# An attention and mixture-of-experts kernel: the first expert's weights get a room of their own and are fetched in the last pairs, the last pair is worked in two query halves, the last routing and the first swaps move forward

## The chip, the core and the metric

The kernel runs on one core of one Trainium2 chip. The core has five engines with a queue each: TensorE (PE in the rows; its weight loads are PEld), VectorE (DVE), ScalarE (ACT), GpSimd (POOL) and SyncE (SP), which here only issues transfers. They work in parallel and wait for each other by semaphores. Every engine's instructions run in the order in which they were written. PE writes to PSUM, the other engines read it; everything else lives in SBUF. The metric is the device time of one launch in microseconds (us). PE's clock has two levels, 2.4 and 1.2 GHz; "granted clock" 1.00 in a row is the upper, 0.50 the lower.

## What is computed

```python
B, H, S, D = q.shape                       # 8, 8, 576, 64
scores = scale * np.matmul(q, k.transpose(0, 1, 3, 2))
kth = np.partition(scores, -32, axis=-1)[..., -32:-31]
scores = np.where(scores >= kth, scores, -1e9)
attn = softmax(scores)
x = (attn @ v).transpose(0, 2, 1, 3).reshape(B * S, H * D)     # 4608 x 512
do = x @ w_skip > 0
logits = x[do] @ w_gate                    # 8 experts
e = argmax(logits); gate = softmax(logits)[e]
y = gate * (relu(x[do] @ w1[e]) @ w2[e])   # w1 512 x 1024, w2 1024 x 512
out = x;  out[do] = x[do] + y
```

## The kernel before

**Attention.** Two heads are a pair; there are `NP` = 32 pairs, four to a batch. A pair's 576 query rows are nine row tiles of 64 rows with both heads side by side (`NR` = 9; tile 8 is the remainder). Its steps, with lines:

- `load_raw`, `load` (L79 to 84, L487): SP loads raw k and q; `load_v` (L497 to 508): SP loads V twice, as `VG` for the values and as `vraw` for the gate.
- `prep` (L541): PE transposes raw into PSUM, ACT copies it to `TT` (L563, L565, "put"), and SP copies halves of `TT` into `TS` with the heads' partitions exchanged ("swap", L581 for k, L583 for q). Row tiles with an odd number take their operands from `TS`, the even ones from `TT`.
- `rows` (L604): PE forms scores (L616), two row tiles to a PSUM tile `r`; ACT copies them to `XC` (L641; tile 8 L643; remainder columns L625).
- `row`, per row tile: DVE takes the top eight of seven chunks (L683) and ranks candidates (L689, L691) to get a first threshold `cl`; ACT writes signs (L696); POOL pushes the wanted scores to `xw` (L699, "push") and fills its end (L703); DVE takes the maxima of that window (L712, "window"), of which the eighth is the exact threshold `wn`; the mask row `PEN` is written by ACT (L709) or, for tiles 2 and 6, by POOL (L707, `PENS`).
- `units` (L742): per 128 keys PE forms the scores again, transposed (L757), and adds the masks (L750); ACT takes the exponential into `PTM` (L788; remainders L791, L794). Every unit waits for all nine mask rows of the pair.
- `heads` (L808): PE multiplies with V (L831, L838); DVE divides by the sums (L841, L867, L844) and adds to the router's logits (L848 to L854); SP stores the result twice (L888, L889), in the last pair ACT's queue does.

**Routing.** When a group of batches (0 to 3, 4 to 6, 7) is ready, `route` (L354 to 478) computes skip, expert, gate and rank of each token with many small operations, then one-hots (`rrh` L459 to L464, `rlo` L468), and PE turns them into the token lists (L474), which DVE adds to `LS` (L477).

**Experts.** `make_room` (L1038) opens the tiles of the first expert in space that the attention gives back. Then, for expert 0, SP fetches four quarters of w1 (`fetch`, L927, 512 KB each) and later four of w2 into the raw tiles; each quarter is split into a rounded high part by ACT (`part_hi`, L930) and a low part, raw less high, by POOL for w1 and DVE for w2 (`part_lo`, L933). POOL gathers the tokens (L994); `turning` transposes them on PE (L1013), ACT rounds (L1017), DVE forms the low part (L1021). An up-product (L1076 to L1078) or down-product (L1099 to L1101) is three matmuls, high by high, low by high and high by low; ACT and DVE apply relu between them (L1081, L1084). The first two blocks of 128 tokens (`EARLY`) start before the last group is routed, with 224 columns; the third follows the last list with 128 columns. The other experts run in a loop behind that.

**Order.** A planner (`Plan`, L150 to 262) writes the instructions. Every task has an engine, an estimated duration, tasks that it needs, and a due number; `when(p, kind, j)` = 9p + `K[kind]` + `FINE[kind][j]`. The planner simulates the engines; of the tasks that could start first on an engine it takes the one with the smallest due number, and waits up to `LOOK` of a duration for a task that is `GAIN` more urgent. The first run of the planner orders the attention, the first two routings, and the first expert's w1 and tokens up to `turning`; the second run (`pl.run()` after L1112) orders the last routing, both blocks' products and the w2 parts.

## Time and profile before

| | before |
|---|---|
| runs | 1092.0, 1093.87, 1099.29 us (median 1093.87) |
| the profiled execution | 1102.62 us, span 1100.7 us, mean granted clock 0.961 |
| PE | 1028.4 us busy (93%) |
| DVE | 907.6 us busy (82%) |
| ACT | 862.4 us busy (78%) |
| POOL | 717.2 us busy (65%) |

Busy shares are means over stages with different limits: attention until about 800 us, experts behind it. All times within the kernel are counted from the start of the span. In a row of the timeline, "x4" means four like instructions in a run; "[2.88 <-DVE hl L1084]" means that the engine was idle for 2.88 us before and that the work named released it. `SPq` and `ACTq` are issues of transfers on these queues; "(xN)" in a window is the number of instructions that touch it.

### The profile page before, as it was taken

What the parts mean: (1) busy time and instruction counts of PE and PEld (TensorE: products, weight loads), DVE (VectorE), ACT (ScalarE), POOL (GpSimd) and SP (SyncE); (2) the same over time, 40 slices, a digit from 0 to 9 for tenths busy, and PEclk for the clock granted to TensorE, in tenths of its full rate; (3) what the DMA queues carried; (4) which work ended last, traced back from release to release, by engine and by line L of the source; (5) the groups of instructions that cost most, each with busy time, mean ns of one, the idle gap of its engine ahead of it and who ended that gap; (6) DMA issues with size and microseconds to landing.
All of it is one profiled execution on the core that took longest, in us unless ns stands there. A gap on an engine that the chain in (4) does not pass through costs nothing.

```text
span 1100.7 us, 40070 instructions
## 1 busy us (share of the span) xinstructions
PE 1028.4 (93%) x14912; PEld 731.9 (66%) x14912; DVE 907.6 (82%) x4910; ACT 862.4 (78%) x1542; POOL 717.2 (65%) x1079
## 2 busy tenths in 40 slices
PE   6799999999999999999999999998868799999996
PEld 3366666666666666666666666665648798889995
DVE  3999999999999999999999999997844365675661
ACT  4899999999999999999999999997842244334450
POOL 2778787888788878888688999887970131111111
PEclk9799999999999999999999999998987689999998
DMA  5333434444443444444344443432147265455620
GB/s 112 88 69 84 95 83 97 105 94 94 96 91 83 104 103 97 90 94 90 83 103 96 96 94 89 99 83 51 40 136 228 68 202 168 145 172 183 202 85 28
DMA packets 290092, 116.15 MB, mean 106 GB/s; under 512 B 258920, under 2 KB 275304, under 8 KB 289888
## 3 DMA queue, kind: packets, MB, share of 16 engines
q1 hardware_dynamic: 282288, 103.13, 38.5%
q0 software_dynamic: 3360, 9.47, 2.5%
q8 instruction: 119, 1.95, 0.7%
q10 hardware_dynamic: 4240, 0.90, 0.4%
q14 instruction: 85, 0.70, 0.2%
HBM read 76.91 MB, written 24.53 MB: 92 GB/s over the span
## 4 chain that ended last, share of the span: by engine, by line
PE 39%; DVE 33%; POOL 13%; ACT 7%; issue 4%; DMA 3%; SPq 1%; POOLq 0%; ACTq 0%; DVEq 0%
DVE cand L683 12%; DVE wn L712 9%; POOL xw L699 7%; PE r L616 4%; DVE cand L691 4%; DVE cl L689 4%; PE r L757 4%; PE ph L1076 4%; PE ph L1077 4%; PE ph L1078 4%; PE py L1099 4%; PE py L1101 4%; PE py L1100 4%; ACT r L696 3%; POOL xw L703 3%
## 5 line engine op out<-in xcount | busy, mean ns | idle before, releaser
L699 POOL TENSOR_TENSOR xw<-XC,r 128x576 f32<-128x576 f32 x288 | 365.2, 1283 | 98.8 <-ACT r L696 72.5
L683 DVE MAX8 cand<-XC 128x8 f32<-128x82 f32 (+1 forms) x2016 | 362.1, 229 | 19.1 <-ACT XC L641 18.8
L712 DVE MAX8 wn<-xw 128x8 f32<-128x585 f32 x288 | 215.5, 760 | 24.4 <-POOL xw L703 21.2
L696 ACT ACTIVATE r<-XC,cl 128x576 bf16<-128x576 f32 x288 | 224.5, 788 | 5.1 <-DVE cl L689 4.1
L616 PE MATMUL r<-TT 64*64 64x64 f32 (+1 forms) x1280 | 203.6, 432 | 0.2 <-ACT PTM L788 0.2
L709 ACT ACTIVATE PEN<-XC,wn 128x576 bf16<-128x576 f32 x224 | 170.2, 785 | 7.7 <-DVE wn L712 7.4
L616 PE MATMUL r<-TS 64*64 64x512 f32 (+1 forms) x1024 | 169.1, 425 | 3.7 <-DMA TS<-TT 3.7
L757 PE MATMUL r<-TT 64*128 64x512 f32 x512 | 150.1, 664 | 16.1 <-ACT XC L643 13.3
L689 DVE MAX8 cl<-cand 128x8 f32<-128x28 f32 (+2 forms) x864 | 153.0, 191 | 0.8
L788 ACT ACTIVATE PTM<-r,top 128x1024 f32<-128x1024 f32 x128 | 140.4, 1125 | 6.4 <-PE r L750 6.2
L641 ACT ACTIVATE XC<-r 128x1024 f32<-128x1024 f32 x128 | 132.1, 1035 | 14.6 <-PE r L616 14.4
L930 ACT ACTIVATE hi<-raw 128x1024 fp32r<-128x1024 f32 x64 | 67.4, 1056 | 74.4 <-PE py L1101 60.9
L750 PEld LDWEIGHTS <-PEN 64*128 64x128 bf16 (+1 forms) x2880 | 70.9, 100 | 76.7 <-issue 74.1
L933 DVE TENSOR_TENSOR lo<-raw,hi 128x1024 fp32r<-128x1024 f32 x60 | 73.5, 1224 | 54.1 <-ACT hi L930 53.5
L707 POOL TENSOR_SCALAR PEN<-XC,wn 128x576 bf16<-128x576 f32 x64 | 110.9, 1733 | 9.2 <-DVE wn L712 4.5
L703 POOL TENSOR_SCALAR xw<-wo,CN 128x9 f32<-128x9 f32 x288 | 99.3, 345 | 26.0
L691 DVE MATCH_REPLACE8 cand<-cl,cand 128x28 f32<-128x28 f32 (+1 forms) x576 | 101.7, 180 | 0.0
L1076 PE MATMUL ph<-xh,hi 128*128 128x224 f32 (+4 forms) x288 | 92.1, 320 | 8.8 <-DVE xb L844 5.9
L1077 PE MATMUL ph<-xl,hi 128*128 128x224 f32 (+4 forms) x288 | 91.5, 318 | 0.3 <-DVE xl L1021 0.3
L1078 PE MATMUL ph<-xh,lo 128*128 128x224 f32 (+4 forms) x288 | 91.3, 317 | 0.0
L994 POOL DMA_INDIRECT xg<-xd,idx x21 | 24.6, 1171 | 101.4 <-DVE ot L1000 87.5
L831 PEld LDWEIGHTS pt<-VG,PTM 128*64 128x64 f32 x2112 | 73.1, 137 | 23.5 <-issue 12.3
(264 smaller groups left out, 2072.2 us busy)
## 6 DMA issues: line engine op xcount, KB each, us to landing
raw<-in_moe_w_dram SPq DMA_DIRECT2D x64, 512.0 KB, 3.8
TS<-TT SPq DMA_DIRECT2D x64, 144.0 KB, 2.5
raw<-in_k_dram SPq DMA_DIRECT2D x64, 128.0 KB, 2.9
VG<-in_v_dram SPq DMA_DIRECT2D x64, 128.0 KB, 2.6
vraw<-in_v_dram SPq DMA_DIRECT2D x64, 128.0 KB, 2.6
raw<-in_q_dram SPq DMA_DIRECT2D x62, 128.0 KB, 3.2
xd<-xb SPq DMA_DIRECT2D x62, 128.0 KB, 2.4
out_dram<-xb SPq DMA_DIRECT2D x62, 128.0 KB, 2.4
```

The costliest lines, as they stand in the source:

```text
L616: nc.tensor.matmul(o[hs_(h)], q_, (ts[src, u:w] if y else tt[src, 0, u:w]), start=True, stop=True)
L683: nc.vector.max(C_[:, c], xc[:, CH[c]:CH[c + 1]])
L689: nc.vector.max(L[:, 4 * r:4 * r + 8], c)
L691: nc.vector.match_replace(c, L[:, 4 * r - 4:4 * r + 4], c, LOWEST)
L696: nc.scalar.activation(rr_, xc, AF.Sign, bias=CL[p % 2][:, t, 23:24], scale=-ODD, accum_out=CN[:, s:s + 1])
L699: nc.gpsimd.tensor_tensor(xw[:, 0:S], xc, rr_, op=OP.mult)
L709: nc.scalar.activation(pen, xc, AF.Relu, bias=WN[p % 2][:, t, 7:8], scale=-1.0)
L712: nc.vector.max(WN[p % 2][:, t], xw)
L757: nc.tensor.matmul(rb[:, 512 * h:512 * h + MAIN], tt[hs_(h), 0, REM + P * kc:REM + P * (kc + 1)], tt[hs_(h), 1, REM:S], start=True, stop=True)
L788: nc.scalar.activation(ptm(kc), H_[kc].t, AF.Exp, bias=nb, scale=scale)
L1076: nc.tensor.matmul(ph[:, u:w], h1[:, c], xh[:, c, u:w], start=(c == 0), stop=False)
L1077: nc.tensor.matmul(ph[:, u:w], h1[:, c], xl[:, c, u:w], start=False, stop=False)
```

## The change

It has five parts. (1) New numbers in `K` and `FINE`, `LOOK`, `GAIN`, `KEEP`, new start times of the engines and estimates of a few durations; a fixed step of 1.0 between the routing's tasks; a routing falls due 30 after its pair's output, and the last one at −5000, ahead of everything on its engines that could run at the same time. (2) Pair 0 takes its row tiles in the order 8, 0, 2, 4, 6, 1, 3, 5, 7, with two even or two odd tiles to a PSUM tile; even ones don't wait for the swaps; the first six chunks of a tile don't wait for the copy of the remainder columns; the loads of V of pairs 0 and 1 and of the gate's weights wait for the first swaps. (3) The first expert's raw weights have permanent tiles, `WA` (four quarters of w1) and `WB` (four of w2), paid for by one buffer less in pool `wk` and by the former pool `ld`; SP fetches them in pairs 23 to 30, one quarter a pair; w1's low parts are formed by DVE; w2's low parts take the tiles `WA` once w1 is split. (4) The last pair's units, exponentials and values run in two halves of four row tiles (the second with tile 8); the first half waits for four mask rows; in the last pair only tile 2's mask row is POOL's; its values use the PSUM tiles `pt`/`pa`, the first tokens' transposes `r`; its result for the tokens' table is stored per head on ACT's queue and the output on SP's. (5) The code for an overflowing expert (which doesn't run with these inputs) reads through `WB`.

The core of the diff:

```diff
-LOOK, GAIN, KEEP = 0.040, 18.850, 0.005
-K = dict(ld=-283.586, turn=-81.069, put=-192.582, swap=-247.941, rr=-119.986,
+LOOK, GAIN, KEEP = 0.027, 36.005, 0.000
+K = dict(ld=-546.563, turn=-120.465, put=-237.977, swap=-421.948, rr=33.73,
...
+    quarter = lambda i, dt=F32: cp.tile([P, CC * F // 4], dt, name=f"wa{i}")
+    WA, WB = [quarter(i) for i in range(4)], cp.tile([P, 4, CC * F // 4], F32, name="wb")
...
-    ld = att.enter_context(tc.tile_pool(name="ld", bufs=2))
-    wk = att.enter_context(tc.tile_pool(name="wk", bufs=2))
+    wk = att.enter_context(tc.tile_pool(name="wk", bufs=1))
...
-    pl.at.update(ACT=4.4, DVE=6.0, POOL=10.5, SP=0.35)
+    pl.at.update(ACT=4.6, DVE=5.6, POOL=5.2, SP=3.1)
...
-        RLOADED[p] = pl.add("SP", 2.0, NR * p + K["lr"], g, VTURNED.get(p - 1), lag=1.5)
-        VLOADED[p] = pl.add("SP", 2.0, NR * p + K["lv"], f, AVF.get(p - 2), lag=1.5)
+        first = READY[0][1] if p < 2 else None
+        RLOADED[p] = pl.add("SP", 2.5, NR * p + K["lr"], g, VTURNED.get(p - 1), first, lag=1.5)
+        VLOADED[p] = pl.add("SP", 2.5, NR * p + K["lv"], f, AVF.get(p - 2), first, lag=1.5)
...
+        both = ((0, 1), (2, 3), (4, 5), (6, 7)) if p else ((0, 2), (4, 6), (1, 3), (5, 7))
...
-            x = A("PE", 0.909 if i < NM else 1.01, when(p, "qk", i), lambda i=i, h2=h2: main(i, h2), puts, sw if i < NM else None, take=h2, mode=ROWS_)
+            x = A("PE", 0.909 if i < NM else 1.01, when(p, "qk", i), lambda i=i, h2=h2: main(i, h2), puts, sw if i < NM and (both[i][0] % 2 or both[i][1] % 2) else None, take=h2, mode=ROWS_)
...
-        for t in ORDER_:
+        for t in range(NR) if p else (8, 0, 2, 4, 6, 1, 3, 5, 7):
             row(p, t)
...
+        pens_ = PENS if p < NP - 1 else PENS[:1]
...
+    PARTS_ = ((0, 4), (4, 8))
...
+        for g, (t0, t1) in enumerate(G):
+            fin = t1 == 2 * NM
+            n = t1 - t0
+            pd = PENNED[p][t0:t1] + (PENNED[p][t1:] if fin else [])
+            for kc in range(NM + 1 if fin else NM):
+                x = A("PE", (1.174 if n > 4 else 0.12 + 0.132 * n) if kc < NM else 1.045, when(p, "unit", kc) + 20 * g, (lambda kc=kc, g=g: main(kc, g)) if kc < NM else rest, pd, TOPPED[p], TU.get(p - 1),
+                      take=H_[g][kc] if kc < NM else hr, mode=UNITS_)
...
-                route(bs, wk, due + K["rt"], RW if end else BT)
+                route(bs, wk, due + 30.0, RW if b == B - 2 else BT)
...
+    FETCHED = {(w, i): pl.add("SP", 0.5, NR * (NP - 9 + 4 * w + i) - K["ld"], lambda w=w, i=i: fetch(0, w, i), LOADED[0, NP - 9 + 4 * w + i], lag=6.0)
+               for w in range(2) for i in range(4)}
     for i in range(4):
-        x = pl.add("SP", 0.3, D0 + 0.1 * i, lambda i=i: fetch(0, 0, i), room, lag=6.0)
-        x = pl.add("ACT", 0.9, D0 + 1 + i, lambda i=i: part_hi(0, i), x)
-        PARTED.append(pl.add("POOL", 2.4, D0 + 1 + i, lambda i=i: part_lo(0, i, nc.gpsimd), x))
+        x = pl.add("ACT", 1.06, D0 + 1 + i, lambda i=i: part_hi(0, i), room, PENNED[NP - 1], FETCHED[0, i])
+        PARTED.append(pl.add("DVE", 1.22, D0 + 1 + i, lambda i=i: part_lo(0, i), x))
...
-    route(GROUPS[-1], mp, D1 - 60, PX)
+    route(GROUPS[-1], mp, -5000.0, PX)
...
+    def low(i):
+        WLO[1][i] = quarter(i, F32R)
+        part_lo(1, i)
     for i in range(4):
-        x = pl.add("SP", 0.3, D1 + 0.1 * i, lambda i=i: fetch(0, 1, i), lag=6.0)
-        x = pl.add("ACT", 0.9, D1 + 6 + 0.1 * i, lambda i=i: part_hi(1, i), x)
-        w2p.append(pl.add("DVE", 1.13, D1 + 6 + 0.1 * i, lambda i=i: part_lo(1, i), x))
+        x = pl.add("ACT", 1.06, D1 + 5.9 + 0.1 * i, lambda i=i: part_hi(1, i), FETCHED[1, i])
+        w2p.append(pl.add("DVE", 1.22, D1 + 5.9 + 0.1 * i, lambda i=i: low(i), x))
...
-    next1 = [pl.add("SP", 0.3, D1 + 1 + 0.1 * i, lambda i=i: fetch(1, 0, i), PARTED[i], lag=6.0) for i in range(4)]
+    next1 = [pl.add("SP", 0.3, D1 + 1 + 0.1 * i, lambda i=i: fetch(1, 0, i), lag=6.0) for i in range(4)]
```

What this does to the order of instructions is shown at three places. First, SP at the start of the program. Before, its first issues are these (`VG` and `vraw` are V, `GW` the gate's weights; the rows of V are four for each `VG` and four for `vraw`):

```order
L84 DMA rawr<-in_k_dram 64x2x64
L503 DMA VG_128<-in_v_dram 128x4x64
L504 DMA VG_128<-in_v_dram 64x64
...
L507 DMA vraw<-in_v_dram 128x4x64
L508 DMA vraw<-in_v_dram 64x64
...
L503 DMA VG_129<-in_v_dram 128x4x64
L504 DMA VG_129<-in_v_dram 64x64
L296 DMA GW<-in_moe_w_gate_dram 64x4x8
L581 DMA TS_102<-TT_99 64x576 x2
L583 DMA TS_102<-TT_99 64x4x64 x2
```

and with the change these:

```order
L85 DMA raw_85<-in_k_dram 128x4x64 x2
L86 DMA rawr<-in_k_dram 64x2x64
L85 DMA raw_85<-in_k_dram 128x4x64 x2
L86 DMA rawr<-in_k_dram 64x2x64
L586 DMA TS_104<-TT_101 64x4x64 x2
L584 DMA TS_104<-TT_101 64x576 x2
L85 DMA raw_86<-in_q_dram 128x4x64 x2
L86 DMA rawr<-in_q_dram 64x2x64
L505 DMA VG_130<-in_v_dram 128x4x64
```

The first swaps now stand behind the loads of k of pairs 0 and 1 alone, q's before k's, and V comes behind them. Second, ACT at the end of the last pair (`PEN` are mask rows, `PTM` and `PR` the exponentials, `hi` the high parts of w1). Before:

```order
L709 ACTIVATE PEN_117<-XC_115,wn_185 128x576 x4
L788 ACTIVATE PTM_123<-r_145,top_142 128x1024
L788 ACTIVATE PTM_122<-r_147,top_142 128x1024
L788 ACTIVATE PTM_118<-r_146,top_142 128x1024
L930 ACTIVATE hi_15696<-raw_15692 128x1024
L794 ACTIVATE PR_127<-r_145,top_142 128x576
L930 ACTIVATE hi_15697<-raw_15693 128x1024
```

and with the change:

```order
L802 ACTIVATE PTM_125<-r_147,top_144 128x2x256
L802 ACTIVATE PTM_124<-r_149,top_144 128x2x256
L716 ACTIVATE PEN_119<-XC_117,wn_187 128x576
L802 ACTIVATE PTM_120<-r_148,top_144 128x2x256
L802 ACTIVATE PTM_121<-r_147,top_144 128x2x256
L716 ACTIVATE PEN_119<-XC_117,wn_187 128x576 x2
L963 ACTIVATE hi_15630<-wa_60 128x1024
L809 ACTIVATE PR_129<-r_149,top_144 128x256
```

The first half's four exponentials stand ahead of the last mask rows, and the high parts read the permanent tiles `wa`. Third, PE where the last group's list is made (`rlo` and `rrh` are its one-hots, `py` the down-products of expert 0, `xg` gathered tokens). Before:

```order
L1100 MATMUL py_16038<-lo_16000,hh_16008 128x512
L1101 MATMUL py_16038<-hi_15996,hl_16016 128x512
L474 LDWEIGHTS rlo_16226
L474 MATMUL px<-rrh,rlo_16226 128x72
...
L1013 MATMUL px<-identF,xg_15704 128x128 x4
L1013 MATMUL px<-identF,xg_16017 128x128 x4
L1076 MATMUL ph<-xh_15705,hi_15696 128x128
```

and with the change:

```order
L1135 MATMUL py_16045<-hi_15639,hl_16020 128x512
L476 LDWEIGHTS rlo_16243
L476 MATMUL px<-rrh,rlo_16243 128x72
...
L1133 MATMUL py_16046<-hi_15639,hh_16012 128x512
L1134 MATMUL py_16046<-wa_16090,hh_16012 128x512
...
L1045 MATMUL px<-identF,xg_15642 128x128 x4
L1133 MATMUL py_16046<-hi_15641,hh_16016 128x512
...
L1045 MATMUL px<-identF,xg_16025 128x128 x4
L1110 MATMUL ph<-xh_15643,hi_15630 128x128
```

Before, the list's five products follow the last down-product of the two blocks and nothing stands between them and the next transposes; with the change 24 matmuls of down-products stand behind the list, 21 of them ahead of the first transposes.

## Rows read from the trace of the kernel before

**Rows 1.** Windows: stretch, us, busy PE, PEld, DVE, ACT, POOL; clock, DMA share, GB/s.

```profile
100.00:400.00 300.00, 291.82 (x5253) 189.47 (x5251) 292.38 (x1820) 297.17 (x544) 244.26 (x357) 1.00 0.43 95
```

**Rows 2.** The page: costliest groups, then DMA issues (KB each, us to landing).

```profile
L699 POOL TENSOR_TENSOR xw<-XC,r 128x576 f32<-128x576 f32 x288 | 365.2, 1283 | 98.8 <-ACT r L696 72.5
TS<-TT SPq DMA_DIRECT2D x64, 144.0 KB, 2.5
raw<-in_moe_w_dram SPq DMA_DIRECT2D x64, 512.0 KB, 3.8
```

**Rows 3.** Timeline of the start: start, duration, operation, idle before and releaser.

```profile
11.76 1.20 SPq L581 DMA_DIRECT2D TS<-TT  x2
8.49 0.60 ACT L563 ACTIVATE TT<-pt 128x512 f32<-128x512 f32 x1 [1.04 <-PE pt L558]
11.01 3.89 PE L616 MATMUL r<-TT 64*64 64x512 f32 x12
13.24 0.65 ACT L643 ACTIVATE XC<-r 128x576 f32<-128x576 f32 x1 [1.57 <-PE r L616]
18.13 1.12 DVE L683 MAX8 cand<-XC 128x8 f32<-128x83 f32 x7 [12.53 <-ACT XC L641]
```

**Rows 4.** Timeline of POOL and DVE ahead of the last window.

```profile
793.36 1.73 POOL L707 TENSOR_SCALAR PEN<-XC,wn 128x576 bf16<-128x576 f32 x1
796.48 0.61 POOL L468 TENSOR_SCALAR rlo<-i,rank 128x128 bf16<-128x128 f32 x1
800.04 1.44 DVE L712 MAX8 wn<-xw 128x8 f32<-128x585 f32 x2 [1.28 <-POOL xw L703]
```

**Rows 5.** Timeline from the last window to the first up-product.

```profile
801.37 2.08 PE L757 MATMUL r<-TT 64*128 64x512 f32 x4
808.06 1.01 POOL L994 DMA_INDIRECT xg<-xd,idx  x1 [0.17 <-issue]
814.33 0.19 POOL L852 COPY lgr<-xb 64x9 f32<-64x9 f32 x1 [4.80 <-DMA xg<-xd,idx]
814.76 9.29 POOL L933 TENSOR_TENSOR lo<-raw,hi 128x1024 fp32r<-128x1024 f32 x4
815.03 0.69 DVE L1021 TENSOR_TENSOR xl<-pt,xh 128x512 fp32r<-128x512 f32 x1 [12.09 <-ACT xh L1017]
816.66 7.44 DVE L848 TENSOR_TENSOR lg<-lg,xb 128x36 f32<-128x36 f32 x1
818.01 0.69 PE L831 MATMUL r<-VG,PR 128*64 128x74 f32 x16
825.20 0.53 PE L1076 MATMUL ph<-xh,hi 128*128 128x224 f32 x1 [5.92 <-DVE xb L844]
```

**Rows 6.** Timeline of the first up-products and what they wait for.

```profile
804.04 36.14 SPq L927 DMA_DIRECT2D raw<-in_moe_w_dram  x16
833.78 1.06 ACT L930 ACTIVATE hi<-raw 128x1024 fp32r<-128x1024 f32 x1 [1.92 <-DMA raw<-in_moe_w_dram]
835.56 0.56 PE L1076 MATMUL ph<-xh,hi 128*128 128x224 f32 x1 [2.88 <-DVE hl L1084]
845.43 0.40 PE L1099 MATMUL py<-hi,hh 128*128 128x512 f32 x1
```

**Rows 7.** Timeline of PE from the last list to the next block.

```profile
856.36 0.34 PE L474 MATMUL px<-rrh,rlo 128*128 128x72 bf16 x5
863.18 1.09 PE L1013 MATMUL px<-identF,xg 128*128 128x128 f32 x4 [0.81 <-DMA xg<-xd,idx]
```

**Rows 8.** Windows of the hand-over and of the experts' loop.

```profile
798.00:801.00 3.00, 0.00 (x0) 0.00 (x0) 1.64 (x4) 0.16 (x2) 2.73 (x5) 0.93 0.15 34
858.00:861.00 3.00, 0.00 (x0) 0.00 (x0) 2.48 (x15) 0.00 (x0) 2.30 (x3) 1.00 0.19 53
864.00:876.00 12.00, 12.00 (x59) 12.00 (x58) 3.78 (x7) 3.77 (x8) 0.00 (x0) 0.50 0.17 54
892.00:1060.00 168.00, 168.00 (x988) 152.82 (x987) 106.64 (x179) 73.13 (x108) 36.15 (x31) 1.00 0.57 181
```

More of the change, by code (lines that the diff above doesn't have):

```diff
@@ new lines @@
+LOOK, GAIN, KEEP = 0.027, 36.005, 0.000
+DRAIN, TURN = 0.11, 28700.19
+K = dict(ld=-546.563, turn=-120.465, put=-237.977, swap=-421.948, rr=33.73, rc=-49.731, qk=42.376, copy=-177.435, chunk=76.184, step=11.097, cand=-62.556, cstep=-187.113, sign=-8.081, fill=-185.335, push=-553.097, window=-5.964, pen=333.292, top=-210.867, flag=-156.199, unit=143.314, exp=-190.441, f1=70.038, f5=-98.317, lg=-208.068, co=298.059, ce=-33.501, rt=406.078, rd=63.598, rs=-191.199, moe=493.198, vt=-35.892, vp=-215.869, vg=-230.983, lv=-174.638, lr=-8.41)
@@ L38 @@
+RS = 1.0
 FILLS = True
@@ L745, in units @@
         A = pl.add
+        end = p == NP - 1
         TU[p] = []
```

162 lines of the change are left out of this document (88 added, 74 removed).

## The prediction

> **What bounds the kernel now.** I read the page first, then windows, the timeline, the chain of waits. The attention stage, from about 30 to 755 us, is full on three engines at once: over 100 to 400 us ScalarE (ACT) is busy 297.17 of 300 us, VectorE (DVE) 292.38, TensorE (PE) 291.82 at the full 2.4 GHz clock [rows 1]. Reordering can win back at most ACT's idle share there, about 1 us per 100. GpSimd (POOL), 244 of 300, is off this bound, but its pushes stand in the chain between the sign and the window. After the attention only PE matters: from 892 to 1060 us it is busy all the time at granted clock 1.00 [rows 8], and the change leaves that loop's matmuls as they are. So time can come only from three places: the start, the hand-over from the last pair to the first expert (790 to 864 us), and the two stretches there that run at the lower of the clock's levels (1.2 GHz).
>
> **Basis.** The durations are from one execution of 1102.6 us (span 1100.7); the median of the runs is 1093.87, 8.7 less. I sum against the former and take the 8.7 off at the end.
>
> **The change, part by part.**
>
> *Start (−4, ends −1 and −6).* The first DVE chunk starts at 18.13, behind a copy of two tiles, one of which comes from the swap; SP issues that swap only at 11.76, behind twelve issues for V and one of gate weights, although the half it copies is in TT at 8.49 + 0.60 = 9.1 [rows 3]. The change takes tile 8 and then the even tiles first, which need no swap. Tile 8's products took 11.01 to 13.24 (2.2 us) and its copy 0.65 [rows 3], so the first chunk can start at 9.1 + 2.2 + 0.65 + 0.2 of hand-over = 12.2, 5.9 earlier. The next piece is two tiles from TT alone, twice tile 8's products: at most 4.4 us and some 1.0 of copy, there at 11.3 + 4.4 + 1.0 = 16.7 at worst. DVE's seven chunks take 1.12 [rows 3] and the five steps behind them about as much again, so it is through with tile 8 at some 14.4. Two of the 5.9 us go to that gap: −4. If the swaps are still what holds it, −1 is left; without a gap −6.
>
> *Tail of the queue ahead of the last window (−2.3, ends 0 and −3.5).* Among its last five pushes POOL runs one mask row (1.73 us) and one one-hot for a list (0.61); DVE then waits 1.28 us for the last fill [rows 4]. The mask row goes to ACT and the list's one-hots go behind the fills: 1.73 + 0.61 = 2.3 less on POOL. It is zero if DVE's own windows, two of them in 1.44 us, are late instead.
>
> *Last window to first up-product: 801.48 to 825.20 = 23.7 now, 18.5 after (−5, ends −2 and −7).* PE stands still from 798 to 801 [rows 8] because every unit waits for all nine mask rows; units and values then run from 801.37 to 818.7 [rows 5]. In halves, the first half needs four mask rows only and can run in that hole. Behind the last window there remain a mask row (0.7), and of the 17.3 us of units and values somewhat over half, since the half-size pieces end with the same hand-over to ACT and back: I take 11, so 11.7 instead of 17.2. Then 7.44 us go in which the logit addition on DVE stood until POOL's four subtractions ended (both at 824.1) [rows 5], since the subtractions move to DVE. But two things become late next. First, the token gather: the order places ten one-hots and two list products on POOL ahead of the last list, twelve operations of about 0.61 [rows 4]; so 7.4 us after the last window the list can be added, and with one subtraction on DVE (about 1.2: half of POOL's 9.29 / 4 = 2.3 [rows 5], an estimate) and about 1.1 for the indices the gather starts at 9.7. Issue and landing took 808.06 to 814.33 = 6.3 [rows 5], so it lands at about 16, and transposing and rounding up to the end of the low part took from there to 815.03 + 0.69 = 1.4 [rows 5] for one block, some 1 more for the second: 18.4. Second, four subtractions of 1.2 on DVE, hidden beside this chain. I take 18.5, hence −5; −7 is the chain without the second block's wait, −2 one in which DVE's subtractions and POOL's one-hots hold each other up for 3.
>
> *Up-products of the first block (−7, ends −3 and −8).* 96 matmuls took 825.20 to 845.43 = 20.2 us with a hole of 2.88 us [rows 5, 6]; 224 columns at 2.4 GHz are 0.093 us each, some 0.11 with what lies between, 10.4 in all. The hole goes back to ACT waiting 1.92 us for a weight transfer, since SP issues sixteen transfers one behind the other over 36 us [rows 6]. The other 7 us are half clock ahead of the hole and behind it. With weights already in SBUF there is neither wait nor a second fall: 10.4 us and 3 of half clock at the front (about half of the 7), 13.4.
>
> *Gap of the last gather (−5, ends −3 and −6).* Now the last list's matmul is PE's last work ahead of the next block: it starts at 856.36, takes 0.34, and the second transpose starts at 863.18, released by the gather [rows 7]: 6.5 us with little in them. After the change 24 down-products stand behind the list matmul, 21 of them ahead of the first transpose; 512 columns at 2.4 GHz are 0.21 us, so 5.1 us of PE work cover the chain and some 1.4 remain. It is −3 if PE now waits at the list matmul, because the routing chain on DVE is interleaved with subtractions of w2.
>
> *The 128-column block behind it (0, or −12).* The next 96 matmuls run at granted clock 0.50, which is 1.2 GHz, 59 of them in 12 us [rows 8]: about 0.21 each. I leave that as it is.
> The profile shows PE at 0.00 busy from 858 to 861, still granted 1.00, and at 0.50 from 864 to 876 although it is busy for all of these 12 us [rows 8]. The Trainium skill ("TensorE: Matmul & The Clock Gate", section "What's actually happening") says that throttled is the default and that activity releases it. By that rule alone a busy stretch would soon get its clock back and the term would be smaller than 12 in either case; the 12 us above disagree, so what matters here is not to fall.
>
> *Steady stage (+1, ends 0 and +4).* Eight fetches of 512 KB move into pairs 23 to 30 on SP. Each takes 3.8 us to land, a swap 2.5 [rows 2]. The DMA engines are at 43% [rows 1], and the fetches are placed five to ten issues ahead of the next pair's swaps. I take +1; one swap late by 3.8 is +4. The new tables reorder every queue, but a pair's order on PE and ACT reads nearly alike: 0.
>
> *At nothing.* The loads of V and of the gate weights now wait for the first swaps; behind them on SP stand the loads of pair 1, which PE needs only after pair 0's products, and the work that fills that time is DVE's nine rows; without that cover it costs the twelve issues that stood ahead of the swap, 8.7 us at most (the 11.76 of [rows 3] less some 3 for the loads ahead). The output stores of the last pair go to SP behind ACT's queue, beside PE's loop. The second expert's first weights no longer wait for the subtractions, but for the fetch of their own room, with three blocks of PE work ahead of their use.
>
> Sum: −4 − 2.3 − 5 − 7 − 5 + 0 + 1 = −22.3, from 1102.6 to 1080.3; less 8.7: **1071.6**.
>
> **The rivals.**
> 1. *Full clock through the 128-column block.* With 1.4 us of hole, PE may never fall: the shortest hole here behind which the rows show a fall is 2.88 us [rows 6]. Against it: the gather's landing decides, and half the down-products stand behind a list that may itself be waited for. It saves 96 × (0.21 − 0.11) = 10 and some 2 of the 512-column products behind them: **1059.6**. Chance 0.25.
> 2. *Port collision.* DVE's addition with both inputs in SBUF stood 7.4 us while POOL worked on SBUF [rows 5]; the subtractions are of that kind and now run while POOL runs ten one-hots. What was won from the stall is given back: +7.4, **1079**. Against it: the low parts have some slack beside the gather chain. Chance 0.14. The Trainium skill ("SBUF — State Buffer", section "Who interferes with whom") says such an instruction and a POOL instruction that reads SBUF lock each other out for a whole instruction, by order of issue; the trace agrees, and shows more: the wait lasted over three whole POOL instructions of 2.3 us, not one.
> 3. *Fetches and the tables eat it.* One swap late by 3.8 us and every gain at its lower end: −1 − 0 − 2 − 3 − 3 + 4 = −5, **1089**, within 1%. Chance 0.13.
> 4. *Other side: a lost place in the steady order.* If the new numbers put each pair's chain behind one more push, the full engines stand 1.28 us [rows 2] in each of about 28 pairs: +35.8 − 22.3 = +13.5, **1107**. It decides from 0.8 us per pair on (22.3/28). Against it: the order of a pair reads alike before and after, and ACT, full, hides a push while it has queued work. Chance 0.06.
>
> **Numbers.** Forecast 0.42, own range 1066 to 1076. 1% is 11 us, about what a measurement of this kernel tells from no change: bounds 1083 and 1105. Faster: the forecast, 1 and 2 (0.81, near the bound so 0.80); within: 3 and an overshoot of 2 (0.14); slower: 4 (0.06). The range 1053 to 1086 takes in the forecast, rivals 1 and 2 with the upper ends of their terms and part of 3.
>
> **What would show it.** In the profile after: first DVE chunk at about 12.2; no PE hole between units of the last pair; first up-product 18.5 us behind the last window; 96 of them in 13 to 14 us with no hole; transposes about 1.3 us behind the last down-product; granted clock 0.50 (forecast) or 1.00 (rival 1) in the 128-column block; DVE's subtractions at about 1.2 us (forecast) or stretched by POOL's (rival 2); ACT at 99% in 100 to 400 us and the last window some 6 us earlier than 801.5. A last window later than 801.5 would make the prediction wrong, as would a list matmul that PE waits for.

## The result, and the profile after

The changed kernel takes 1061.28 us (median of 4 runs, 1058.62 to 1062.52), the kernel before 1094.07 beside it; the ratio is 0.969, 95% interval 0.965 to 0.973: 3.1% faster. The forecast was 1071.6 in a range of 1053 to 1086, so the time lies in the range, 10 us below the likeliest case and 2 us above the value of the first rival (1059.6). That it comes so near the rival is partly luck: the rival's gains sum to 34.3 us (22.3 and 12), the traces differ by 6.5 more, and the 8.7 taken off for the basis make up for it.

The profiled execution of after took 1061.84 us (span 1059.9), that of before 1102.62; they differ by 40.8 us, the medians by 32.8. The kernel before was therefore profiled a second time (below). By stretches, in us:

| stretch | before | before, second | after | moved | forecast |
|---|---|---|---|---|---|
| start to the end of the last window | 801.5 | 803.7 | 789.4 | −12.1, −14.3 | −5.3 (−4 −2.3 +1) |
| to the first up-product | 23.7 | 18.7 | 20.4 | −3.3, +1.7 | −5 |
| to the end of the up-products | 20.2 | 18.6 | 14.0 | −6.2, −4.6 | −7 |
| to the 128-column block | 18.5 | 18.3 | 11.3 | −7.2, −7.0 | −5 |
| that block | 22.1 | 22.0 | 12.0 | −10.0 | 0 (rival: −10) |
| to the end of the span | 214.7 | 214.5 | 212.8 | −1.9, −1.7 | 0 (rival: −2) |

In the second trace of before the first up-product stands earlier but alone: the second waits 4.23 us more for the low part.

```profile
827.00 0.56 PE L1077 MATMUL ph<-xl,hi 128*128 128x224 f32 x1 [4.23 <-DVE xl L1021]
```

Counted from the last window to the second up-product the two traces of before and that of after took 24.5, 23.3 and 20.7 us, and from there to the end of the up-products 19.4, 14.0 and 13.7. The hole of 2.88 us [rows 6] and the half clock behind it are in the first trace of before and not in the second, although ScalarE waits 6.15 us for a transfer of weights there too. So these 5 us did not belong to every execution of the kernel before. In all, the second trace is 4.9 us shorter: 6.8 less from the last window to the 128-column block (62.4 and 55.6 us), and 2.2 more ahead of it.

Page and windows of after, as [rows 1] and [rows 8] (columns as there). The steady stage is as full as before; the hole ahead of the up-products is there (806 to 809), half clock behind it (810 to 814), but from 826 to 847, gap and 128-column block, PE is at 1.00 and busy but for 0.23 us:

```profile
PE 1004.0 (95%) x14932; PEld 714.4 (67%) x14932; DVE 898.6 (85%) x4914; ACT 862.2 (81%) x1548; POOL 706.7 (67%) x1074
100.00:400.00 300.00, 292.88 (x5281) 190.46 (x5279) 291.72 (x1815) 297.82 (x546) 247.41 (x355) 1.00 0.43 95
806.00:809.00 3.00, 0.14 (x2) 0.00 (x0) 0.73 (x2) 1.23 (x3) 0.00 (x0) 0.78 0.85 183
810.00:814.00 4.00, 4.00 (x20) 4.00 (x21) 3.34 (x8) 2.93 (x5) 0.00 (x0) 0.50 1.07 349
826.00:835.00 9.00, 9.00 (x48) 7.26 (x48) 4.69 (x27) 0.60 (x1) 4.10 (x4) 1.00 0.26 71
836.00:847.00 11.00, 11.00 (x102) 11.00 (x101) 7.04 (x12) 6.04 (x13) 0.00 (x0) 1.00 0.31 102
```

The start, as [rows 3]: the swap is issued at 8.72 instead of 11.76, and DVE has its first copy at 13.00 instead of 18.13 (11.84 to 13.38 in the other executions of this order). That copy is of two even tiles, not of tile 8, whose copy follows at 13.22:

```profile
8.72 1.32 SPq L586 DMA_DIRECT2D TS<-TT  x2
11.95 1.02 ACT L647 ACTIVATE XC<-r 128x1024 f32<-128x1024 f32 x1 [3.61 <-PE r L619]
13.00 2.17 DVE L690 MAX8 cand<-XC 128x8 f32<-128x83 f32 x13 [7.39 <-ACT XC L647]
```

From the last windows to the first up-product, as [rows 4] and [rows 5]. PE waits for one-hots of the last list, one by one (794.8 to 797.3, only the last shown); the second gather lands at 805.48; ScalarE issues four stores (804.49 to 807.67) and only then rounds the tokens:

```profile
787.92 1.44 DVE L719 MAX8 wn<-xw 128x8 f32<-128x585 f32 x2 [1.02 <-POOL xw L710]
788.41 2.92 POOL L470 TENSOR_SCALAR rlo<-i,rank 128x128 bf16<-128x128 f32 x5
793.38 3.67 POOL L470 TENSOR_SCALAR rlo<-i,rank 128x128 bf16<-128x128 f32 x5
797.11 0.21 PE L476 MATMUL r<-rrh,rlo 128*128 128x72 bf16 x1 [0.37 <-POOL rlo L470]
805.48 0.66 PE L1045 MATMUL r<-identF,xg 128*128 128x128 f32 x4 [0.79 <-DMA xg<-xd,idx]
809.75 0.56 PE L1110 MATMUL ph<-xh,hi 128*128 128x224 f32 x1 [3.61 <-DVE xl L1053]
804.49 1.60 ACTq L906 DMA_DIRECT2D xd<-xb  x2
807.77 1.08 ACT L1049 ACTIVATE xh<-r 128x512 fp32r<-128x512 f32 x2 [5.14 <-DMA xd<-xb]
```

The last list and what follows, as [rows 7]: the list's products at 827.86, down-products behind them, a transpose at 833.60 in the middle of these, and the next block's products with a wait of 0.23 us where 6.5 had been:

```profile
827.86 0.34 PE L476 MATMUL px<-rrh,rlo 128*128 128x72 bf16 x5
833.60 0.60 PE L1045 MATMUL px<-identF,xg 128*128 128x128 f32 x4
835.61 0.33 PE L1111 MATMUL ph<-xl,hi 128*128 128x128 f32 x1 [0.23 <-DVE xl L1053]
```

### The profile page after: what moved, and what is told of

It reads as the page before. It is cut to its first block, busy times and chain, and to the rows that moved or that the text cites. A ratio compares the mean times of both kernels' runs of the same rounds, so it can differ in the third digit from the quotient of the medians.

```text
span 1059.9 us, 40100 instructions
## 1 busy us (share of the span) xinstructions
PE 1004.0 (95%) x14932; PEld 714.4 (67%) x14932; DVE 898.6 (85%) x4914; ACT 862.2 (81%) x1548; POOL 706.7 (67%) x1074
## 3 DMA queue, kind: packets, MB, share of 16 engines
q8 instruction: 120, 1.97, 0.8%
## 4 chain that ended last, share of the span: by engine, by line
PE 54%; DVE 14%; POOL 13%; ACT 11%; issue 4%; DMA 2%; SPq 1%; ACTq 0%; POOLq 0%; DVEq 0%
PE r L619 7%; POOL xw L706 7%; PE r L767 6%; DVE cand L690 6%; PE pa L850 5%; PE pt L850 4%; PE ph L1110 4%; PE ph L1111 4%; PE ph L1112 4%; DVE wn L719 3%; PE py L1133 3%; PE py L1135 3%; ACT r L703 3%; PE py L1134 3%; POOL xw L710 2%
## 5 line engine op out<-in xcount | busy, mean ns | idle before, releaser
L719 DVE MAX8 wn<-xw 128x8 f32<-128x585 f32 x288 | 215.0, 760 | 16.6 <-POOL xw L710 13.4
L619 PE MATMUL r<-TT 64*64 64x64 f32 (+1 forms) x1280 | 198.8, 426 | 1.6 <-ACT PTM L800 0.8
L619 PE MATMUL r<-TS 64*64 64x512 f32 (+1 forms) x1024 | 158.8, 422 | 3.1 <-DMA TS<-TT 3.1
L696 DVE MAX8 cl<-cand 128x8 f32<-128x42 f32 (+2 forms) x864 | 158.1, 191 | 0.9
L767 PE MATMUL r<-TT 64*128 64x512 f32 (+1 forms) x528 | 147.8, 638 | 9.2 <-ACT XC L649 7.4
L800 ACT ACTIVATE PTM<-r,top 128x1024 f32<-128x1024 f32 x124 | 137.3, 1123 | 4.0 <-PE r L758 3.9
L850 PEld LDWEIGHTS pa<-VG,PTM 128*64 128x64 f32 x2048 | 72.6, 138 | 28.1 <-ACT PTM L800 5.7
L619 PEld LDWEIGHTS r<-TT 64*64 64x64 f32 x1280 | 59.5, 134 | 45.2 <-issue 29.0
L1110 PE MATMUL ph<-xh,hi 128*128 128x224 f32 (+4 forms) x288 | 85.9, 298 | 3.6 <-DVE xl L1053 3.6
L850 PE MATMUL pt<-VG,PTM 128*64 128x74 f32 x2048 | 83.3, 232 | 3.5 <-DVE xb L863 1.7
L850 PE MATMUL pa<-VG,PTM 128*64 128x74 f32 x2048 | 83.8, 232 | 2.8 <-DVE xb L863 1.7
L1026 POOL DMA_INDIRECT xg<-xd,idx x21 | 23.3, 1112 | 93.9 <-DVE ot L1032 85.3
```

What stands on the lines that cost most here:

```text
L619: nc.tensor.matmul(o[hs_(h)], q_, (ts[src, u:w] if y else tt[src, 0, u:w]), start=True, stop=True)
L696: nc.vector.max(L[:, 4 * r:4 * r + 8], c)
L719: nc.vector.max(WN[p % 2][:, t], xw)
L767: nc.tensor.matmul(rb[:, 512 * h + u:512 * h + w], tt[hs_(h), 0, REM + P * kc:REM + P * (kc + 1)], tt[hs_(h), 1, REM + u:REM + w], start=T ...
L800: nc.scalar.activation(o_.rearrange("p h c -> p (h c)"), i_, AF.Exp, bias=nb, scale=scale)
L850: nc.tensor.matmul(h.t[hs_(t % 2), VW * (t // 2):VW * (t // 2 + 1)], w, vg[:, a, kc], start=(kc == 0 and t < 2), stop=(kc == NM), skip_gro ...
```

## Experiments

Ratios are to the kernel before on the same chip, with 95% intervals; medians of the changed kernel were 1061.28 and 1062.05. The kernel before is the unsteadier of the two (1088.6 to 1107.4 over all runs, its medians 1094 to 1100), while the runs of one version of the changed kernel mostly lie within 4 us. Versions of the changed kernel are therefore compared by their medians first, and where the ratios say otherwise, that is said. Executions of one order differ within the attention too: pair 16 takes 24.3 us in most traces of the changed order and 25.9 or 26.0 in three.

**The kernel before again.** No edit.

> The kernel before, unchanged, for a second profiled execution. In the first one the last window of the last pair ended at 801.5 us, 12.1 us later than in the changed kernel (789.4), where the forecast had some 6, and the row of pair 30's last reduction stood 39.8 us behind that of pair 29 where a pair takes about 24. Theory A (the stall between 754 and 768 us, where the swaps of pair 31 are issued behind loads of V and stores, is fixed in the order of the program): the stall is there again, last window at 799 to 803, ratio 1.00. Theory B (it belongs to that execution, whose time was 8.7 us above the median): it is smaller or gone, last window near 793 to 796, ratio 1.00 too.

Ratio 0.997 (0.994 to 1.000), median 1096.53. The last window ended at 803.7. The reductions that close pairs 29 and 30, first and last start in the row (first of before, then of the second profile, then of after):

```profile
L671 DVE TENSOR_REDUCE top<-cl x2: 160/160/161, 731.4 to 771.2; 128x1 f32<-128x9 f32 x2
L671 DVE TENSOR_REDUCE top<-cl x2: 160/160/160, 733.2 to 773.5; 128x1 f32<-128x9 f32 x2
L677 DVE TENSOR_REDUCE top<-cl x2: 150/157/164, 728.0 to 754.2; 128x1 f32<-128x9 f32 x2
```

39.8 and 40.3 us apart, 26.2 in after: theory A, the stall of pair 30 belongs to the order of the program. The pair behind it takes 20.5 us before and 27.2 in after, so over the three pairs 29 to 31 the changed kernel is 8.5 us shorter.

**That stall, by SP's queue.** The swaps of pair 31 go ahead of V of pair 30 and of the stores of pair 28 (`HELD`), in the kernel before:

```diff
+        if p == NP - 2:
+            load(p + 1)
+            prep(p + 1)
+            HELD.pop()(READY[p + 1][1])
...
-        VLOADED[p] = pl.add("SP", 2.0, ..., AVF.get(p - 2), lag=1.5)
+        VLOADED[p] = pl.add("SP", 2.0, ..., AVF.get(p - 2), READY[p + 1][1] if p == NP - 2 else None, lag=1.5)
```

> The kernel before with one thing moved on SP: the swaps of pair 31 are issued ahead of the load of V of pair 30 and of the stores of pair 28, behind which they stood; everything up to there keeps its order. In the kernel before the halves lie in TT at 749.4 and 751.3, the swaps are issued at 751.5 and 756.4, and PE takes up the swapped half at 758.6, after which it runs 6 us at half clock and ACT and DVE wait 3 to 4 us. Theory A (SP's queue makes that stall): the swapped half is there 4 to 5 us earlier, no half clock from 760 to 766, last window 4 to 8 us earlier, time -4 to -8 against before, ratio 0.993 to 0.996. Theory B (the transposes on PE and the routing's work stand too late in the order, SP adds little): last window 0 to 2 earlier, ratio 0.998 to 1.001.

The pair shrank as theory A had it, the last window ended at 797.8 (4 to 6 earlier), but the time did not move: ratio 1.000 (0.997 to 1.004).

```profile
L671 DVE TENSOR_REDUCE top<-cl x2: 158/161/164, 733.0 to 768.6; 128x1 f32<-128x9 f32 x2
813.44 5.06 DVE L848 TENSOR_TENSOR lg<-lg,xb 128x36 f32<-128x36 f32 x1
830.38 0.37 PE L1087 MATMUL ph<-xh,hi 128*128 128x224 f32 x1 [3.71 <-DVE hl L1095]
```

The first up-product came 21.8 us behind the last window, the logit addition stood 5.06 us, and PE waited 3.71 us at the third group of up-products. That the hand-over took the gain back is likely, not shown: from the last window to the 128-column block it took 59.8 us, between the 62.4 and 55.6 of the two traces of before. Nor did the edit act on SP alone: behind it, in the last pair, the planner put GpSimd's last mask row behind the fills, and the last window follows the last reduction by 8.1 us instead of 9.7. And SP's queue is not the whole stall: 35.6 us remain of 40.

**Numbers of the tables alone.** The changed kernel with the old `LOOK`, `GAIN`, `KEEP`, `TURN`, `K`, `FINE`.

> The changed kernel with the numbers of the kernel before in K, FINE, LOOK, GAIN, KEEP and TURN; all structural parts of the change stay. Theory A (the forecast: the tables are worth about nothing in the steady stage, 0 with 6 either way): the reductions of pairs 3 to 28 stand within 6 us of those of the changed kernel, the time within 6, ratio 0.963 to 0.975. Theory B (the tables fit this structure and take the stall of pairs 30 and 31 away, which cost the kernel before 12 us over two pairs of 24): that stall is there again or others are, time +8 to +16, ratio 0.976 to 0.984.

Ratio 1.022 (1.019 to 1.026), median 1121: 59 us slower than the changed kernel, far beyond either theory. Two stalls make most of it, at pair 5 (54.2 us) and pair 23 (63.4 us; the pair behind each takes 9.5, so some 41 us in all), in which PE waits for what stands too late on the other engines. The rows are from pairs 23 and 24:

```profile
590.72 0.76 PE L676 MATMUL pa<-shift,top 128*128 128x128 f32 x2 [7.62 <-ACT r L703]
599.86 2.08 PE L767 MATMUL r<-TT 64*128 64x512 f32 x4 [5.49 <-ACT XC L649]
663.26 2.08 PE L767 MATMUL r<-TT 64*128 64x512 f32 x4 [8.66 <-ACT XC L649]
```

So the old numbers don't fit the new structure. What the new numbers do in the old structure was not run, so the worth of the tables and that of the structure cannot be told apart.

**Stores of the gates later (a new order).** `due + 0.9` becomes `due + 900` for the first two routings.

> The changed kernel with the stores of the gates of batches 0 to 6 due 900 later, so that SP takes them when it has nothing else. In the changed kernel pair 20 takes 28.9 to 31.0 us where its neighbours take 23 to 25: SP issues eight gate stores (5.2 us) at 481.7 to 490.4, the loads of the next k and q stand behind them, and PE waits 4.4 us for the k it is to transpose, loses its clock, and DVE and ACT wait 4 us each. Theory A (these stores cause it): the stall of pair 20 is gone, last window 3 to 7 us earlier, time -3 to -7 against the changed kernel. Theory B (PE's order or the transposes cause it, SP is only the last to be seen, or the new order loses as much elsewhere): within 2.

Ratio 1.007 (1.003 to 1.011), 43 us slower than the changed kernel. Pair 20 lost its stall as theory A had it, but the planner made another order, in which PE waits for the lists' one-hots in pair 26 (68.7 us, the next 13.3). The reductions of pairs 19 and 20 in after and here, those of pairs 25 and 26 here, and the wait:

```profile
L677 DVE TENSOR_REDUCE top<-cl x2: 153/155/157, 477.9 to 508.9; 128x1 f32<-128x9 f32 x2
L677 DVE TENSOR_REDUCE top<-cl x2: 150/150/151, 478.8 to 503.1; 128x1 f32<-128x9 f32 x2
L677 DVE TENSOR_REDUCE top<-cl x2: 146/153/160, 626.5 to 695.2; 128x1 f32<-128x9 f32 x2
634.97 0.24 PE L476 MATMUL pa<-rrh,rlo 128*128 128x72 bf16 x1 [7.72 <-POOL rlo L470]
```

**The same with the order kept.** Each gate store is held back until the pair's four swaps are written; only SP's queue changes.

```diff
+        if b < B // 2 and FIRST:
+            return [pl.add("SP", 1.35, due, lambda x=x: PEND.append(lambda: f(*x)), after, lag=2.5) for x in whats]
...
+        def swap_then(u, w):
+            swap(u, w)
+            left[0] -= 1
+            while not left[0] and PEND:
+                PEND.pop(0)()
```

> The changed kernel with one thing moved on SP and the order of all other engines unchanged row by row: the eight gate stores of batches 0 to 3 are issued behind the loads of k and q and the swaps of the pair ahead of which they stood. It repeats the question of a_gate without its new order (there pair 20 took 24.3 instead of 31.0 us, but a new order of the lists made PE wait for GpSimd in pair 26 and cost 45). Theory A: the stall of pair 20 is gone, 4 to 7 us, and the gain stays through to the end: last window 4 to 7 earlier, time -4 to -7, ratio to before 0.961 to 0.965. Theory B (a later place takes it back, as a gain of 5 in pair 30 of the kernel before was taken back behind the last window): last window earlier, time within 2.

Median 1058.36, 3 to 4 below the changed kernel; ratio 0.966 (0.960 to 0.973), which does not tell it from 0.969. The rows show the cause: in after, k of the next pair is issued at 490.45, behind the last gate store, and PE waits 4.42 us; here pair 20 has 24.3 us again (pairs 19 and 20 in the last row).

```profile
489.77 0.64 SPq L354 DMA_DIRECT2D xd<-gt  x1
490.45 1.29 SPq L85 DMA_DIRECT2D raw<-in_k_dram  x2
494.63 0.45 PE L561 MATMUL pt<-identF,rawr 128*128 128x128 f32 x1 [4.42 <-issue]
L685 DVE TENSOR_REDUCE top<-cl x2: 147/152/156, 479.1 to 503.4; 128x1 f32<-128x9 f32 x2
```

But pairs 21 and 22 take 28.4 and 26.1 us instead of 25.1 and 24.2, so of the stall's 6.7 us only 1.5 are left behind pair 22; pair 16, which the edit doesn't touch, took 26.0 here, and the last window ends at 789.0, as in after: theory B. The first up-product came 2 to 3 us earlier than in after, because the clock did not fall at the lists in this execution (1.00 from 798 to 801, 0.53 in after), though PE waited for the one-hots as long; how much of the 3 is the stall stays open.

**The fetches back at the end.**

```diff
-    FETCHED = {(w, i): pl.add("SP", 0.5, NR * (NP - 9 + 4 * w + i) - K["ld"], ..., LOADED[0, NP - 9 + 4 * w + i], lag=6.0)
+    FETCHED = {(w, i): pl.add("SP", 0.5, D0 + 10 * w + 0.1 * i, ..., room, lag=6.0)
```

> The changed kernel with the eight fetches of the first expert's weights issued when the tiles of the first expert open, as before, in place of pairs 23 to 30; the order on the other engines is the same row by row. Theory A (the early fetch is what removes the hole of 2.9 us and the second stretch at half clock among the up-products): the hole is back at the high parts of w2, time +4 to +8. Theory B (what helps is the room alone, since eight fetches of 512 KB issued at about 790 us still land before 810): within 1.5 of the changed kernel. On the steady stage: if the fetches cost the pairs 23 to 30 anything, as the lag of 8 us that the changed kernel builds up against the one before between pairs 19 and 28 might say, last window 2 to 6 us earlier; if not, last window unchanged within 1 us.

Median 1060.66, within 1 us of the changed kernel; by the ratio, 0.964 (0.960 to 0.968), it may be up to 5 us ahead of it, but not behind. Theory B, though not at the times that it names: SP issued the four fetches of w1 and the first of w2 from 770.6 on and the last three from 786.5, the kernel before its first at 804.04 [rows 6]. ScalarE never waits for one, and the up-products have no hole; the second trace of before has none either, so the hole alone proves little. So room is what they need: five of the eight fetches at 13 to 16 us ahead of the last window's end and three right at it are early enough. Eight fetches from 790 on were not tested. The last window ended 2.6 us earlier than in after, but 2.1 of these fall on pair 20, which lies ahead of every fetch in after. From pair 22 to pair 28 the reductions are 148.6 us apart here and 149.1 in after, so the early fetches cost about 0.5, not the 8 us by which the changed kernel falls back between pairs 19 and 28; of these, 5.8 fall on pair 20.

**w1's low parts on GpSimd again.** `part_lo(0, i)` becomes `part_lo(0, i, nc.gpsimd)`.

> The changed kernel with the low parts of w1 formed by GpSimd again, behind the first gather. Theory A (moving them to VectorE removed a stall of 7.4 us at the logit addition): the addition stands again until GpSimd's four subtractions (2.3 us each) end, the first up-product comes 4 to 8 us later, time +4 to +8. Theory B (the gather and the queue of stores on ScalarE set the first up-product anyway, at 809.7): 0 to +2.

Median 1068.35; 6 to 7 above the changed kernel and 7.7 above the late fetch, which ran beside it on the same chip, as theory A (the ratio of 0.970, 0.966 to 0.974, rests on 1099.6 for before and would give 1 to 2). The first up-product came 28.2 us behind the last window instead of 20.4. On DVE one addition of 64x9 lasts 6.89 us, and ends as GpSimd's subtractions end (814.61); the copy behind it lasts 2.28 us, until the three memsets that GpSimd runs next have ended (816.91):

```profile
807.75 6.89 DVE L869 TENSOR_TENSOR lg<-lg,xb 64x9 f32<-64x9 f32 x1 [4.93 <-POOL lg L873]
814.65 2.28 DVE L871 COPY lgr<-xb 64x9 f32<-64x9 f32 x1
807.68 6.93 POOL L966 TENSOR_TENSOR lo<-wa,hi 128x1024 fp32r<-128x1024 f32 x3
```

**The last pair in one piece.** `PARTS_ = ((0, 8),)`.

> The changed kernel with the last pair's units, exponentials and values in one piece again; no other order changes before that pair. In the changed kernel the values end 14.5 us behind the last window (803.9 - 789.4), of which 2.4 us are spent at the second list's products, each waiting for a one-hot of GpSimd; the forecast had 11.7. Theory A (halves are worth what the forecast says, units no longer wait for nine mask rows): the first up-product comes 3 to 6 us later, time against the changed kernel +3 to +6, ratio to before 0.972 to 0.976. Theory B (the end is set by the one-hots, the list and the gather, not by the units): 0 to +1.5, ratio 0.969 to 0.971.

Median 1065.07 (1060.94 to 1067.15): 3 to 4 above the changed kernel by the medians, and 4.4 above the late fetch on the same chip, but not above it by the ratio (0.967, 0.962 to 0.971). In the traces the values end 18.8 us behind the last window instead of 14.5, and the first up-product comes at 23.0 instead of 20.4: 2.6 us. That is a little less than theory A has and more than theory B; the times alone don't settle it.

**The last routing late again.** Due `D1 - 60` and 3.66 a step; only the list's place on PE moves.

> The changed kernel with the last routing due as before (not ahead of everything, 3.66 between its steps); the only difference in the order is on PE: the last list's five products stand behind nearly all down-products of the first two blocks again instead of 24 matmuls ahead of their end. Theory A (the covered gap keeps PE busy, and being busy keeps the upper clock for the 128-column block): PE stands idle 4 to 6 us ahead of the block, the block runs at granted clock 0.50, its 96 matmuls 0.21 apart (some 10 us more), time +12 to +18 against the changed kernel. Theory B (the clock there has nothing to do with the gap): only the hole is back, +4 to +6, granted clock 1.00.

Median 1080.09, ratio 0.986 (0.980 to 0.993): 18 to 19 us above the changed kernel. Theory A, by the windows: 0.35 us of work in 5 us ahead of the block, then 20 us without a gap at 0.50, from 841.95 to 863.9 for the 96 products:

```profile
835.00:840.00 5.00, 0.35 (x2) 0.39 (x3) 3.35 (x21) 0.00 (x0) 3.10 (x3) 0.87 0.26 57
843.00:863.00 20.00, 20.00 (x97) 20.00 (x96) 7.79 (x13) 5.97 (x12) 0.00 (x0) 0.50 0.18 57
```

The other traces agree: the block took 22.0 to 22.1 us in the four in which PE waited some 5 us for the gather ahead of it (three of them of the kernel before or the version of it above), and 11.6 to 12.0 in all ten in which it did not.

**Two moves at the end of the last pair.** The last list's one-hots on DVE, the stores for the tokens' table on SP.

> The changed kernel with two things moved at the end of the last pair: the one-hots of the last list of the second group are made by VectorE ahead of the last windows (0.22 each there, 0.61 to 0.73 on GpSimd), and the last pair's four stores to the tokens' table are issued by SP, not ScalarE. In the changed kernel PE waits 0.37 to 0.39 for each of five one-hots and loses its clock (794.8 to 797.3), and the rounding of the first tokens stands 5 us behind store issues on ScalarE's queue. Theory A (these two set the first up-product): values end 2 to 4 us earlier, no half clock in the last units, first up-product 4 to 7 us earlier (16 behind the last window instead of 20.4), time -4 to -7, ratio 0.961 to 0.965. Theory B (the gather's landing sets it): -1 to -3.

Neither, by the time: median 1071.95 (1062.36 to 1073.46), ratio 0.980 (0.973 to 0.986). The profiled execution took 1062.36 us; the four others 1071.2 to 1073.5. The hand-over shrank as theory A had it, to 16.3 us from the last window to the first up-product, but the last window ended at 793.3, 4 later, so the first up-product came no earlier (809.6). Of these 4, 3 stand ahead of the last reduction (784.4 instead of 781.3), where neither edit acts; 0.9 lie behind it, where DVE now makes the one-hots: four took 1.97 us while GpSimd pushed, not 0.9. Ahead of the 128-column block PE stood still for 1.7 us of 7, and kept its clock in this execution:

```profile
789.12 1.97 DVE L471 TENSOR_SCALAR rlo<-i,rank 128x128 bf16<-128x128 f32 x4
830.00:837.00 7.00, 5.27 (x33) 4.26 (x32) 3.63 (x17) 1.20 (x2) 4.10 (x4) 1.00 0.42 115
```

The 10 us between the profiled execution and the others are what the block costs at half clock; that they fell there was not profiled, so it is likely, not shown. Their mean granted clock, 0.966 to 0.971 against 0.981, fits it.

**The changed kernel again.** No edit.

> The changed kernel, unchanged, beside the three that follow, and a second profiled execution of it. Expected: ratio to before 0.965 to 0.973, first DVE chunk at 12 to 13 us, last window 787 to 791, granted clock 1.00 through the 128-column block again. If that block shows 0.50, the gain of some 10 us there belongs to the one execution; then the time would be near 1072.

Median 1062.05, ratio 0.968 (0.965 to 0.971); first chunk 11.92, last window 789.9, the block in 12.0 us. As expected.

**A version that beats both.** The held-back gate stores, the table's stores on SP, and matmuls to keep PE busy:

```diff
+    for _ in range(16):
+        nc.tensor.matmul(PY0[1][:, 0:224], WHI[0][0][:, 0:P], WHI[0][0][:, 0:224], start=True, stop=True)
```

> The changed kernel with three things: the gate stores behind the swaps as in a_defer; the last pair's four stores to the tokens' table on SP, not ScalarE (one half of a_tail, without the one-hots on VectorE that delayed the last windows there); and 16 matmuls of 128x224 with no use, written to a bank that the down-products overwrite, put on PE between the first tokens' transposes and the first up-product, where PE stands still for 1.5 to 3.6 us in the changed kernel. Order otherwise unchanged. Theory A (PE falls to 1.2 GHz behind that hole and only there; being busy keeps it up): the 96 up-products and the three down-products among them take 11.5 to 12 us, not 14.0, first up-product 17 to 19 behind the last window, time -5 to -8 against the changed kernel, ratio 0.960 to 0.964. Theory B (the clock had already fallen at the lists' waits, or the useless matmuls only delay the first up-product): stretch of 14 us again, time -2 to -4, ratio 0.964 to 0.968.

Median 1055.58 (1055.06 to 1056.99, 6 runs), ratio 0.959 (0.956 to 0.962): 4.1% faster than before, and ahead of the changed kernel by 6 us by the medians (10 by the ratios). The useless matmuls ran from 803.4 to 806.9, at half clock; from 807 on the up-products have 0.99 (0.50 up to 814 in after):

```profile
803.40 3.49 PE L1139 MATMUL py<-hi 128*128 128x224 f32 x16
804.00:807.00 3.00, 3.00 (x16) 3.00 (x16) 2.66 (x6) 3.00 (x4) 0.00 (x0) 0.50 0.55 114
807.00:810.00 3.00, 3.00 (x28) 3.00 (x28) 1.92 (x5) 1.61 (x5) 0.00 (x0) 0.99 1.00 308
```

From the first up-product to the last list it took 16.0 us, against 18.1 in after. ScalarE rounds the tokens at 803.68, right behind their transpose. Theory A for the clock, but not for the first up-product: it came 20.3 us behind the last window, as in after (20.4), not 17 to 19, because it stands behind the useless matmuls, while the low part of the tokens that it needs had ended at 805.0. From the last window to the last list it took 36.3 us, 38.5 in after and 37.0 with the gate stores held back alone, so the useless matmuls and the table's stores on SP are together worth some 0.7 us net by these traces; neither was run by itself. The last window, at 786.3, was 3 earlier than in after: pairs 20 to 22, where the held-back stores act, took 77.4 us instead of 80.3.

## Why the forecast came out as it did

**What was wrong first: the 128-column block.** The likeliest case left it at half clock, the term was 0; it was −10, with −2 behind it, as the first rival had it. The gap was sized nearly right (1.4 us remaining, 0.23 measured), and it was the gap that decides: with it back the block has 0.50 for all of its 22 us (late routing), without it 1.00. It should have been the forecast, since both were one mechanism; the reason given against it, a gather that lands late, had 5.1 us of cover that held in every profile of the changed order but one, where 1.7 us remained (the two moves). The Trainium skill ("TensorE: Matmul & The Clock Gate", section "What's actually happening") has activity release the throttle; by that rule alone the block of the late routing would have won its clock back. That run disagrees, with 0.50 through 20 us without a gap.

**The start, −4: too small.** By pair 19 the changed kernel is 9.5 us ahead. The first chunk moved by −5.1 (5.9 were worked out). Another 2.6 are idle time of DVE between that chunk and the reduction of pair 0: it was busy for 20.51 of these 24.07 us before and is for 17.71 of 18.68 after. So the two us taken off for a gap were wrong, and a gap of the old order was overlooked: PE waited 2.50 us for k of pair 1 there (22.60), which stood behind the loads of V and now stands ahead of them. That this wait is what DVE idled for was not tested, and of the last 2 us no run here shows the cause.

**The steady stage, +1: near by luck.** From pair 19 to pair 31 it was −0.9 (−2.5 by the second traces of both kernels), as a sum of moves that no term had. The eight gate stores on SP cost pair 20 5.8 us. The fetches, the term itself, cost some 0.5 to 1. And the stall of pair 30 was not in the working at all, because the steady stage was read from the stretch of 100 to 400 us alone [rows 1]: 40 us for a pair of 24, in both traces of before, ahead of the hand-over at which the prediction's rows begin. Without it the changed kernel gains 8.5 us between pairs 28 and 31. Which part of the new order takes the stall away is not settled: SP's queue is 4 to 5 us of it, and the old tables make other stalls. With the start and the tail that is −12 where −5.3 stood, and most of the difference is the start.

**The tail of the queue, −2.3.** From the last reduction to the end of the last window it took 9.7 and takes 8.0: −1.7, near the size worked out. The version of before with the swaps of pair 31 moved has 8.1, and there too the mask row and a list's one-hots stand behind the fills.

**Last window to first up-product, −5.** −3.3 against the first trace and +1.7 against the second, where the first product stood 4.2 us ahead of the second; to the second product it is −3.8 and −2.6. Right: the stall of 7.44 us goes with the subtractions (7 us in the runs), and the gather lands 16.1 us behind the last window, as worked out (about 16). Mis-sized: from there to the end of the low part it took 4.2 us, not 2.4, because ScalarE issues four stores ahead of the rounding (some 2 us), which stood in no term, though they were part of the diff. And the values, which these stores wait for, end after 14.5 us, not 11.7, because PE's queue holds the last list's products, four of them waiting 0.37 us or more for a one-hot, ahead of units and values.

**Up-products, −7.** 14.0 with three down-products of 0.7 among them, so 13.3, as worked out (13.4). But what it was reckoned against, the hole and the second fall of the clock, is in one trace of before and not in the other; there the stretch took 18.6 us only because the second product waited 4.23, and from that product on the change gains 0.3. The reason was half right: weights with room of their own, fetched by the end of the last window, leave no wait; that they are fetched in pairs 23 to 30 is not needed.

**Gap, −5.** −7.2; the list's products were not waited for, and only 0.23 us remained.

**The rivals.** The port collision came small: the subtractions on DVE took 1.23 us each, and five of GpSimd's one-hots took 3.67 us (above) instead of the 2.92 of the five before them. PE takes these five at 0.60 to 0.57 from each other, so the 0.75 fell on the first, which ran beside a subtraction (793.63 to 794.86); the price was paid by the lists. The fetches did not eat the gain. The other side did not come with this order, but its size was no exaggeration: two edits of the planner's numbers cost 43 and 59 us.

**The basis.** 8.7 us were taken off as if they were spread evenly; the second trace is shorter in the hand-over and longer ahead of it. With the second trace as the basis (1097.7), it would have been 3.8 to take off, 4.8 less to win ahead of the first up-product (18.7 there are all but the 18.5 forecast) and 1.8 less in the up-products (18.6 to 13.4): 1097.7 − 15.7 − 3.8 = 1078.2, farther off, since the stall, the rest of the start and the block were still missing.

## What to carry to other kernels

Look at the length of every period of a repeated stage, not at one window of it: one pair of 32 stood 16 us longer than the others, in both traces of before, and the window that was read did not hold it. In a kernel whose queues are written by a planner, test an edit with the order held fixed on the other engines; otherwise the new order is what is measured. Where PE's clock hangs on a gap of a few us, what counts is the work behind the gap: cover the gap with work that is due anyway, as the down-products did here (10 us). Matmuls of no use brought the up-products to 0.99 as well, but the first useful product then waits for them, and some 0.7 us was left of the gain. And profile the kernel before twice: a hole that one trace has may not be in the next.

## What the runs showed of the hardware

A DVE addition of 64x9 took 6.89 us beside three GpSimd subtractions in a row (2.3 each): as in [rows 5], with 7.44 for 128x36, it waited for the whole run of them, not for one. A DVE copy of 64x9 took 2.28 us there, until three memsets of GpSimd had ended, and 1.47 in the run with the gate stores held back, beside one memset of 1.42. PE kept 0.50 through 20 us of gapless 128-column products after a gap of 5 us, and 1.00 through the same products after 0.23 us; after 1.7 us of idle time spread over 7, it kept 1.00 in the one execution that was profiled.
